# Linear attention and MLP layers in fp32r: operand addresses, warming products, half tiles and a new order

## Chip, cores and metric

One core of a Trainium2 chip. The metric is the device time of one execution in microseconds; the kernel before took 888.67 us (median of three runs, 885.83 to 890.14).

## What is computed

Two layers over x of 2,048 rows and 448 columns, each an attention block A and an MLP block B with the same weights in both layers:

```python
x = x + _A_ref(_layernorm(x), A_wqkv, A_wo)   # 16 heads of 28; phi(t) = (t + 1 if t > 0 else exp(t)) + 1e-6
# q, k, v = x @ wqkv; kv = phi(k).T @ v; z = sum phi(k); o = phi(q) @ kv / (phi(q) . z + 1e-6); o @ wo
x = x + _B_ref(_layernorm(x), B_w1, B_b1, B_w2, B_b2)   # gelu(x @ w1 + b1) @ w2 + b2, 1,792 hidden
```

All of it is float32. Products run on TensorE as fp32r (a rounded fp32); to keep the accuracy each operand is split into a high and a low part, and high x high, high x low and low x high are summed.

## The kernel before, in words

x is cut into 16 tiles of 128 rows. 448 columns are three pieces of 128 and a tail of 64; the tail's high and low parts (of the weights, in `w1x` and pieces 6, W6 for wk and V6 for wq) share one piece of 128 rows. For a projection of one tile, `proj` (L486 on) issues eleven products of 448 columns: for each of three pieces high x high (L492), high x low (L493) and low x high (L494), and two for the tail (L496, L497).

The parts of a layer, by the names that the order uses: `ld` loads a tile of x; `a`, `ar`, `n` are the statistics (DVE), the root (POOL, L349) and the normalization (DVE, L353); `d` copies the tail (ACT); `T` turns a tile by four transposes on TensorE into one bank (`tp`, L382), or `tu`, `st`, `sp` turn it on DVE in 32 x 32 squares, store it to DRAM and load it spread; `xh` and `xl` split the turned tile (ACT and DVE); `sh` and `sl` split the tile as it is (ACT, and POOL at L484 and L485). `K` and `Q` are the projections, with `ke`, `kp`, `kh`, `kl`, `za` and `qe`, `qp`, `qs` behind them (exponentials on ACT, the rest on DVE; `qs` stores phi(q) to DRAM). `G` sums x-transposed times phi(k) over all tiles in four banks (eleven products a tile, L566 to L570). `wkld`, `wkh`, `wkl` and `wqld`, `wqh`, `wql` load and split the pieces of wk and wq; `bld`, `bhi`, `blo` those of w1 and w2 (layer 0 only). Behind the last G come the small products (`z`, `gt`, `kv`, `m`), then per tile the division (`pl`, `pz`, `pd`, `pm`), its turning, `o` or `oc` (products with the combined matrix), the second norm, and the MLP: `f` (eleven products of 512 columns for 128 hidden units and four tiles, L799 to L803), `g`, `gh`, `gl` (gelu and its split), `y` (four times three products of 448 columns, L826 to L828, into four banks over 14 `f`), `ya` and `ys` (sum and store).

The order in which all of this is issued is written out by hand, as a list of these names for each layer (`ORDER`): `run` (L853) goes through it and calls the function of each name, with the tile or piece as number. `:p` or `:a` gives the engine, and `>` or `<` takes the name from the next or the former layer, so the layers overlap. Each engine executes its instructions in that order; every wait between engines follows from the tiles. Loads on SP are one queue, in the same order; a few of the first are issued by ACT (`:a`).

Before the first tile is ready, `warm20` issues 20 transposes of a constant, whose results nobody reads.

Tiles are laid out in SBUF in the order of their pools and first uses, each at a multiple of 32 bytes: constants first (from byte 384), then the weights of the MLP (`wts`), then `work`, in which the small tiles of the statistics stand between the large ones. By the sizes, `w1h` starts at byte 5,696, `w2h` at 55,872, XH at 159,040, the rings A, B, E, F, of 2,048 bytes, at 202,560 and on: 64 bytes over a multiple of 256 in each case. The pieces wk 1, 4 and 6 (142,848 and on) and the rings S and e start at a multiple of 256.

PSUM has eight banks: four with the name `acc` (G, y, o), two `h` (f, Q, transposes) and two `m` (K and the small products).

Of the kernel before, what the change touches and what calls it, by code (L numbers as in the profile page):

```python
# [70 lines left out]
    ),  # L71
    (
# [43 lines left out]
def linear_attn_mlp_kernel(  # L116
# [46 lines left out]
    def small(n, name):  # L163
        return work.tile([128, n], F32, name=name, tag=name, bufs=BUFS["small"])
# [51 lines left out]
    @op  # L216
    def warm(l, n, e):
        if (l, "warm") not in T:
            T[l, "warm"] = bank("m", "warm")
        for i in range(n):  # L220
            pe.transpose(T[l, "warm"][:, :128], ident, ident)
# [668 lines left out]
```

## Time and profile before

| what | us |
|---|---|
| median of three runs | 888.67 |
| the profiled execution | 886.11 |
| its span, first to last instruction | 884.4 |
| TensorE busy in the span | 873.2 |
| DVE busy | 473.7 |
| ACT busy | 337.0 |
| POOL busy | 203.8 |

Busy times of TensorE count pipelined products, so its load is better read from the distance between the starts of consecutive instructions. Other engines' busy times are those of one instruction at a time. A row of the timeline gives start, duration, engine, line, operation, out<-in and shape; PEld is the load of a stationary operand, PE the product itself. A row of the stretches gives, for each engine, busy time and number of instructions, then the granted clock of TensorE, the DMA engines' share and GB/s.

### The profile page before, as it was taken

The numbers are of one execution on the slowest core, as the hardware profiler recorded it, in microseconds if no ns is written. First come the engines' busy times: TensorE is split into PE (matmuls) and PEld (weight loads), VectorE is DVE, ScalarE is ACT, GpSimd is POOL, SyncE is SP. The second block draws the span as 40 slices with busy tenths as digits, with TensorE's granted clock in tenths as the row PEclk, the third lists the DMA queues.
The fourth block names the chain that finished last, engine by engine and source line by source line (L and its number), as shares of the span: only waits on it lengthen the run. The fifth ranks groups of instructions, "written<-read, shape, count | busy, mean of one in ns | idle before, by whom it ended". The sixth has DMA issues, their size and how long they took to land.

```text
span 884.4 us, 11576 instructions
## 1 busy us (share of the span) xinstructions
PE 873.2 (99%) x4184; PEld 773.2 (87%) x4184; DVE 473.7 (54%) x970; ACT 337.0 (38%) x594; POOL 203.8 (23%) x239
## 2 busy tenths in 40 slices
PE   8999999999999999999999999999999999999998
PEld 7999888889888888888889898888888888888887
DVE  6877597456555434225468855853754564342212
ACT  5768644323223222324446554342232232223221
POOL 3656543231022002010033323130320230020000
PEclk9999999999999999999999999999999999999999
DMA  4677623522413241141145453134234124020101
GB/s 138 202 229 229 190 80 120 169 90 84 154 36 117 86 145 48 49 136 48 49 135 175 152 153 105 52 104 146 98 101 152 59 82 135 1 96 1 52 1 42
DMA packets 62762, 93.71 MB, mean 106 GB/s; under 512 B 8816, under 2 KB 57968, under 8 KB 62704
## 3 DMA queue, kind: packets, MB, share of 16 engines
q1 hardware_dynamic: 62096, 92.05, 32.5%
q10 hardware_dynamic: 608, 0.92, 0.3%
q8 instruction: 33, 0.54, 0.3%
q14 instruction: 25, 0.20, 0.1%
HBM read 55.65 MB, written 34.08 MB: 101 GB/s over the span
## 4 chain that ended last, share of the span: by engine, by line
PE 93%; DVE 3%; DMA 2%; ACT 1%; issue 0%; POOL 0%; SPq 0%; ACTq 0%; POOLq 0%; DVEq 0%
PE y L828 10%; PE y L827 10%; PE y L826 10%; PE hp L800 9%; PE hp L799 9%; PE hp L801 9%; PE hp L802 3%; PE hp L803 3%; PE psk L492 2%; PE G L567 2%; PE G L568 2%; PE G L566 2%; PE psk L494 2%; PE psk L493 2%; PE psq L493 2%; PE psq L494 2%
## 5 line engine op out<-in xcount | busy, mean ns | idle before, releaser
L818 DVE TENSOR_TENSOR gl<-g,gh 128x512 fp32r<-128x512 f32 x112 | 80.9, 728 | 193.6 <-ACT gh L210 193.4
L828 PE MATMUL y<-w2h,gl 128*128 128x448 f32 x448 | 163.7, 365 | 1.5 <-DVE gl L818 1.5
L827 PE MATMUL y<-w2l,gh 128*128 128x448 f32 x448 | 163.7, 365 | 0.0
L826 PE MATMUL y<-w2h,gh 128*128 128x448 f32 x448 | 163.6, 365 | 0.0
L808 ACT ACTIVATE g<-hp,b1s 128x512 f32<-128x512 f32 x112 | 76.2, 686 | 201.2 <-PE hp L803 183.8
L210 ACT CAST gh<-g 128x512 fp32r<-128x512 f32 x112 | 69.1, 620 | 171.7 <-PE y L827 158.5
L800 PE MATMUL hp<-XH,w1l 128*128 128x512 f32 x336 | 131.2, 390 | 0.0
L801 PE MATMUL hp<-XL,w1h 128*128 128x512 f32 x336 | 131.1, 390 | 0.0
L799 PE MATMUL hp<-XH,w1h 128*128 128x512 f32 x336 | 131.1, 390 | 0.0
L349 POOL TENSOR_TENSOR brs<-bve,mhalf 128x1 f32<-128x1 f32 x64 | 39.2, 616 | 342.4 <-DVE bve L343 342.3
L828 PEld LDWEIGHTS y<-w2h,gl 128*128 128x128 f32 x448 | 84.2, 188 | 8.5 <-DVE gl L818 1.9
L826 PEld LDWEIGHTS y<-w2h,gh 128*128 128x128 f32 x448 | 84.2, 188 | 8.4
L827 PEld LDWEIGHTS y<-w2l,gh 128*128 128x128 f32 x448 | 84.1, 188 | 8.0
L801 PEld LDWEIGHTS hp<-XL,w1h 128*128 128x128 f32 x336 | 63.1, 188 | 13.5
L800 PEld LDWEIGHTS hp<-XH,w1l 128*128 128x128 f32 x336 | 63.1, 188 | 11.8
L799 PEld LDWEIGHTS hp<-XH,w1h 128*128 128x128 f32 x336 | 63.1, 188 | 11.7
L665 POOL TENSOR_TENSOR pz<-pq,zb 128x448 f32<-128x448 f32 x32 | 38.7, 1212 | 100.2 <-DVE dn L670 57.2
L484 POOL TENSOR_TENSOR xnl<-x,xnh 128x384 fp32r<-128x384 f32 x32 | 33.6, 1051 | 68.3 <-ACT xnh L210 48.0
L744 DVE TENSOR_TENSOR x<-op,x 128x448 f32<-128x448 f32 x32 | 19.8, 620 | 51.6 <-PE op L738 50.8
L420 DVE TENSOR_TENSOR XL<-sp,XH 128x512 fp32r<-128x512 f32 x50 | 35.8, 728 | 18.8 <-ACT XH L210 18.8
L339 DVE BATCH_NORM_STATS2 bst<-x 128x6 f32<-128x448 f32 x64 | 39.7, 620 | 9.3 <-DMA x<-in_A_x_dram 5.7
L802 PE MATMUL hp<-XH,w1x 128*128 128x512 f32 x112 | 43.6, 389 | 0.0
(142 smaller groups left out, 1577.2 us busy)
## 6 DMA issues: line engine op xcount, KB each, us to landing
x<-in_A_x_dram SPq DMA_DIRECT2D x32, 224.0 KB, 4.0
pq_d<-eq SPq DMA_DIRECT2D x32, 224.0 KB, 2.6
pq<-pq_d SPq DMA_DIRECT2D x32, 224.0 KB, 3.2
x<-x_d SPq DMA_DIRECT2D x32, 224.0 KB, 2.9
sq_a<-sq SPq DMA_DIRECT2D x13, 512.0 KB, 2.9
sp<-sq_a SPq DMA_DIRECT2D x52, 128.0 KB, 3.2
sq_q<-sq SPq DMA_DIRECT2D x12, 512.0 KB, 2.9
sp<-sq_q SPq DMA_DIRECT2D x48, 128.0 KB, 2.9
```

The source lines that it names most:

```text
L210: act.copy(out, src)
L339: dve.bn_stats(st, xs)
L349: pool.tensor_tensor(rs, ve, mhalf, op=OP.pow)
L799: pe.matmul(o, w1h[:, c, s], x.moving(x.hi, c), start=(c == 0), stop=False)
L800: pe.matmul(o, w1l[:, c, s], x.moving(x.hi, c), start=False, stop=False)
L801: pe.matmul(o, w1h[:, c, s], x.moving(x.lo, c), start=False, stop=False)
L802: pe.matmul(o, w1x[:, s], x.moving(x.hi, 3), start=False, stop=False)
L808: act.activation(T[l, "g", n], T[l, "hp", n], AF.Gelu_apprx_tanh, bias=b1s[:, n % NF:n % NF + 1])
L818: dve.tensor_sub(lo, T[l, "g", n], f(hi))
L826: pe.matmul(o, gh[:, r], w2h[:, i, s], start=first, stop=False)
L827: pe.matmul(o, gh[:, r], w2l[:, i, s], start=False, stop=False)
L828: pe.matmul(o, gl[:, r], w2h[:, i, s], start=False, stop=last)
```

## The change

- **Addresses.** The small tiles of the statistics move to a pool of their own, and a constant tile of 56 floats that nobody uses is added. By the sizes, `wts` then starts at byte 6,432, and as all its tiles and those of `work` are multiples of 256 long, every one of them starts 32 bytes over a multiple of 256.
- **Warming.** `hot16` stands for `warm20`: 16 products of 512 columns with a tile of ones, whose results nobody reads. `ones` becomes fp32r and is set first on POOL.
- **Halves.** Tiles 0 and 1 of layer 0 are turned, split and projected for K in halves (`ht`, `hx`, `hl`, `hk`) of two pieces each, in place of T, xh, xl and K. Each tile's K keeps its eleven products, in another sequence.
- **`fl`**: one more product like those of `hot`, behind the transposes of tile 5 in layer 0.
- **Order.** Both lists are new throughout. At the start `ar0` stands right behind `a0`; wk's low parts 0, 1 and 2 are on DVE and 3 on POOL (before: 1 on POOL); wq's pieces 1 and 3 are loaded by SP and no longer by ACT. Fewer parts of layer 1 stand in layer 0's list.

```diff
-        "ld0 a0 ld1 a1 wkld0 wkld1:a wkld2 wkld3:a wqld0 wqld1:a wkh1 wkl1:p wkh3 ar0 n0 d0 wkh0 ar1 n1 d1 wkl3 "
-        "warm20 wqld2 ld2 wkl0 T0 xh0 xl0 wkh2 wqld3:a tab0 T1 xh1 wqh0 wqh2 sh0 wkl2 K0 xl1 K1 ke0 a2 ar2 wql0 "
-        "wqh1 wql1:p n2 wql2 d2 T2 kp0 wqh3 wql3 Q0 kh0 kl0 ld4 ld3 a4 a3 ke1 sl0 G0 qe0 qp0 qs0 kp1 kh1 xh2 ar4 "
+        "ld0 a0 ar0 ld1 a1 n0 hot16 wkld0 wkld1:a wkld2 wkld3:a wkh1 wkl1 ht0 wkh0 ar1 wkl0 n1 d0 ht1 hx0 hl0 hk0 "
+        "wkh2 wkl2 wkh3 d1 ht3 hx1 hl1 wqld0 wqh0 ht2 hx2 wkl3:p hk1 hx3 hl2 hk2 hl3 wql0 hk3 ld2 wqld1 wqh1 a2 "
+        "ke0 kp0 bld1:xn wqld2 wqh2 wqld3 wqh3 kh0 sh0 wql2 wql3 wql1:p Q0 ar2 n2 d2 T2 sh1 sl0 kl0 G0 ld3 ld7 a3 "
...
+        "ke4 kp4 Q4 kh4 T5 xh5 sp3 blo4 bhi5 blo5 ar11 fl kl4 qs3 xl5 tu10 n11 a9 za4 tu8 G3 G4 bld6:xn bld7:xn "
...
+        ">wkh0 gh52 gl52 y52 >wkl0 >tu3 >wql0 >sp0 >xh0 gh53 g55 g54 gl53 y53 gh54 >st1 gl54 y54 >sh0 >sl0 >xl0 "
+        ">K0 gh55 gl55 y55 >tu4 >xh1 >xl1 ya13 ya12 >ld5 >sp1 lb14 ya14 ys13 ys12 >ld6 ya15 ys15 "
...
+        "ke0 Q0 K1 Q1 xh2 xh3 kp0 kh0 ke1 xl2 a5 ar5 xl3 n5 za0 tu5 qe0 <ys14 ld7 kl0 G0 a6 sh1 qe1 qp1 ld8 st2 "
...
+    smalls = ctx.enter_context(tc.tile_pool(name="smalls", bufs=2))
...
-        return work.tile([128, n], F32, name=name, tag=name, bufs=BUFS["small"])
+        return smalls.tile([128, n], F32, name=name, tag=name, bufs=BUFS["small"])
...
+    ones = consts.tile([128, 128], F32R, name="ones")
+    pool.memset(f(ones), 1.0)
...
+    consts.tile([128, 56], F32, name="pad")
...
+    @op
+    def hot(l, n, e):
+        w = bank(e or "m", "hot")
+        for i in range(n):
+            pe.matmul(w.rearrange("p (r n) -> p r n", r=4), ones, ones[:, None, :].to_broadcast([128, 4, 128]),
+                      start=True, stop=True)
...
+    def ht(l, n, e):
+        t, h = divmod(n, 2)
+        tp = T["tp", ("h", l, n)] = bank(e or "acc", "tp")
+        for c in (2 * h, 2 * h + 1):
+            pe.transpose(tp[:, rows(c % 2)], T["tail", l, t] if c == 3 else T["xn", l, t][:, rows(c)], ident)
...
+    def fl(l, n, e):
+        hot(l, 1, e)
```

`hx` copies one half's 256 columns (ACT), `hl` subtracts them (DVE). `hk` issues six products for the first half (the four high ones, then the two low ones) and five for the second.

More of the change, by code (lines that the diff above doesn't have):

```diff
@@ L177, in linear_attn_mlp_kernel @@
     pool.memset(zc, S * 1e-6)
-    ones = consts.tile([128, 128], F32, name="ones")
-    pool.memset(ones, 1.0)
     mask = consts.tile([G, G], F32, name="mask")
@@ L452, in tu, with hx, hl, hk @@
     @op
+    def ht(l, n, e):
[3 more added lines that the diff above has]
+            pe.transpose(tp[:, rows(c % 2)], T["tail", l, t] if c == 3 else T["xn", l, t][:, rows(c)], ident)
+    @op
+    def hx(l, n, e):
+        t, h = divmod(n, 2)
+        copy(ENG[e or "a"], block("a", l, t // 4).pieces(t % 4)[0][:, h * 256:(h + 1) * 256],
+             T["tp", ("h", l, n)][:, :256])
+    @op
+    def hl(l, n, e):
+        t, h = divmod(n, 2)
+        hi, lo = (x[:, h * 256:(h + 1) * 256] for x in block("a", l, t // 4).pieces(t % 4))
+        dve.tensor_sub(lo, T["tp", ("h", l, n)][:, :256], f(hi))
+    @op
+    def hk(l, n, e):
+        t, h = divmod(n, 2)
+        if h == 0:
+            T["K", l, t] = bank(e or "m", "psk")[:, :D]
+        o = T["K", l, t]
+        b = block("a", l, t // 4)
+        if h == 0:
+            for c in range(2):
+                for w in range(2):
+                    pe.matmul(o, b.still(b.hi, t % 4, c), T[l, "w", "k", c][w], start=(c + w == 0), stop=False)
+            for c in range(2):
+                pe.matmul(o, b.still(b.lo, t % 4, c), T[l, "w", "k", c][0], start=False, stop=False)
+        else:
+            pe.matmul(o, b.still(b.hi, t % 4, 2), T[l, "w", "k", 2][0], start=False, stop=False)
+            pe.matmul(o, b.still(b.hi, t % 4, 2), T[l, "w", "k", 2][1], start=False, stop=False)
+            pe.matmul(o, b.still(b.hi, t % 4, 3), T[l, "w", "k", 3], start=False, stop=False)
+            pe.matmul(o, b.still(b.lo, t % 4, 2), T[l, "w", "k", 2][0], start=False, stop=False)
+            pe.matmul(o, b.still(b.lo, t % 4, 3), T[l, "w", "k", 3], start=False, stop=True)
+    @op
+    def fl(l, n, e):
+        hot(l, 1, e)
+    @op
     def tu(l, t, e):
@@ L587, in z @@
         T[l, "zp"] = bank(e or "m", "zp")[:, :D]
-        pe.matmul(T[l, "zp"], ones, T["za", l], start=True, stop=True)
+        pe.matmul(T[l, "zp"], f(ones), T["za", l], start=True, stop=True)
     @op
```

171 rows, old and new, of the table ORDER are left out of this document.

## The prediction

> **What bounds the kernel now.** I read the page's shares first, then PE's waits, then the starts of PE's instructions in the timeline, since the shares alone say only "PE".
>
> ```profile
> span 884.4 us, 11576 instructions
> PE 873.2 (99%) x4184; PEld 773.2 (87%) x4184; DVE 473.7 (54%) x970; ACT 337.0 (38%) x594; POOL 203.8 (23%) x239
> PE 93%; DVE 3%; DMA 2%; ACT 1%; issue 0%; POOL 0%; SPq 0%; ACTq 0%; POOLq 0%; DVEq 0%
> ```
>
> TensorE is busy 99% and holds 93% of the chain that ended last. It hardly waits: the longest waits on the page of PE's waits are
>
> ```profile
> PE tp L382 <- DVE x L353: 2.8, 1, 2.8
> PE y L828 <- DVE gl L818: 1.5, 1, 1.5
> PE psk L492 <- DVE za L538: 0.8, 1, 0.8
> PE psq L492 <- DVE eq L507: 0.6, 1, 0.6
> ```
>
> 5.7 us in all, half of it before the first projection. So a gain has three places: the start, the few waits, and the distance from one product's start to the next. Four stretches of the timeline give that distance.
>
> ```profile
> 21.29 0.37 PE L492 MATMUL psq<-wq,XH 128*128 128x448 f32 x1
> 23.52 0.36 PE L492 MATMUL psk<-wk,XH 128*128 128x448 f32 x1
> ...
> 65.42 0.37 PE L492 MATMUL psq<-wq,XH 128*128 128x448 f32 x1
> 67.70 0.37 PE L492 MATMUL psk<-wk,XH 128*128 128x448 f32 x1
> 69.94 0.36 PE L492 MATMUL psk<-wk,XH 128*128 128x448 f32 x1
> ...
> 465.57 0.36 PE L492 MATMUL psq<-wq,XH 128*128 128x448 f32 x1
> 467.80 0.36 PE L492 MATMUL psk<-wk,XH 128*128 128x448 f32 x1
> 500.46 0.37 PE L492 MATMUL psq<-wq,XH 128*128 128x448 f32 x1
> 505.01 0.37 PE L566 MATMUL G<-kh,xnh 128*128 128x448 f32 x1
> ...
> 299.69 0.39 PE L799 MATMUL hp<-XH,w1h 128*128 128x512 f32 x1
> 300.39 0.39 PE L799 MATMUL hp<-XH,w1h 128*128 128x512 f32 x1
> 302.20 0.36 PE L826 MATMUL y<-w2h,gh 128*128 128x448 f32 x1
> 305.24 0.39 PE L799 MATMUL hp<-XH,w1h 128*128 128x512 f32 x1
> ```
>
> The same 11 products of a Q take 2.23 us at 21.29 (203 ns each) and 2.28 us at 65.42 (207 ns). There are two steady states: a free one and a **slow lock**. Layer 1 has both too: 2.23 us at 465.57, and 22 products in 4.55 us at 500.46. The K between 67.70 and 69.94 takes 2.24 us. The 15 products of y up to 305.24 take 3.04 us, 203 ns: free. A product of 512 columns starts 233 ns after the last one at first (three in 0.70 us), then 226 (eight in 1.81 us). Free, it costs some 13 ns over its columns (512 are 213 at 2.4 per ns: twice the half-clock rate of the cold rows under the rivals); a 448-column product costs 16 (187 are columns), locked 20. The weight load beside them says why the short ones cost more:
>
> ```profile
> 65.42 0.19 PEld L493 LDWEIGHTS psq<-wq,XH 128*128 128x128 f32 x1
> 65.63 0.37 PE L493 MATMUL psq<-wq,XH 128*128 128x448 f32 x1
> 305.25 0.19 PEld L800 LDWEIGHTS hp<-XH,w1l 128*128 128x128 f32 x1
> 305.47 0.39 PE L800 MATMUL hp<-XH,w1l 128*128 128x512 f32 x1
> ```
>
> Each load starts as the product before it starts, runs 0.19 us, and its own product follows 0.02 us later at 448 columns, 0.03 us at 512. At 448 the load and its hand-over are the bound, at 512 the stream. Without the load's share a 448-column product would start every 200 ns (187 + 13).
>
> **The addresses (the unknown).** Worked out from the tiles' sizes, w1, w2, XH, XL, A, B, E, F, wq and wk 0, 2, 3, 5 now start 64 bytes over a multiple of 256, and wk 1, 4, 6 and the S and e rings at a multiple. Afterwards all start 32 over: the pad and the constants end there, the small tiles fill 512 bytes of their own, and every large tile is a multiple of 256 long. Nothing in this trace starts 32 over, so the price is bounded from rows. The K at 67.70 holds five products with wk 1, 4, 6 at offset 0, the locked Q before it none: 2.24 against 2.28 us. So the offset matters to a locked product, by 40 ns / 5 = 8 ns at most. A free K doesn't show it (from 21.29 on Q and K alike run at 203). Lower end: no 448-column product is bound by its load, 200 ns for 2,760 of them (1,344 y, 360 op, 1,056 psk, psq and G), and the lock is gone. Upper end: every product locked, 207 and 233 ns. I take the middle between 203 and 200 for the plateau, since offsets 0 and 64 are equally near to 32, and the lock gone, since a locked product is where an offset shows:
> - plateau: 2,760 x 1.35 ns = **-3.7 us**;
> - lock: by the starts in between, read in the same way, it holds from 31 to 108 us and from 474 to 541, 145 us or 700 products; a K loses 10 ns and a Q or G 50 ns in 11, on average 37 / 11 = 3 ns: **-2.1 us**;
> - hp: 112 blocks of 11; the block at 299.69 takes 2.51 us, 11 x 226 are 2.49; half of that difference, as the next block is better: **-1.1 us**.
>
> Together -6.9 us; the ends are -12 (2,760 x 2.7 ns + 2.1 + 2.2) and +14 (1,704 x 4 ns + 1,056 x 2 + 1,232 x 4).
>
> Stores and loads of the S ring move from offset 0 to 32 too. The row first, and where it stands on a chain:
>
> ```profile
> sq_a<-sq SPq DMA_DIRECT2D x13, 512.0 KB, 2.9
> ...
> 467.60 5.10 DMA sq_a<-sq
> ```
>
> The Trainium skill, "DMA: Bandwidth & Descriptors", section "How a descriptor splits into AXI transactions", speaks against the change: a transfer is cut at multiples of 256 bytes, so a 4,096-byte row begun 32 over needs 17 pieces instead of 16. By it the one at 467.60 would grow by at most a sixteenth, 0.3 us (an estimate), once, at the layer boundary; no run here shows it. Without it I price them at nothing: most others (x, w) are off a multiple in both kernels.
>
> **The start.**
>
> ```profile
> 5.22 0.63 DVE L339 BATCH_NORM_STATS2 bst<-x 128x6 f32<-128x448 f32 x1 [0.18 <-DMA x<-in_A_x_dram]
> 6.55 1.13 POOL L286 TENSOR_TENSOR wk<-stg,wk 128x448 fp32r<-128x448 f32 x1 [4.06 <-ACT wk L210]
> 7.64 1.14 POOL L349 TENSOR_TENSOR brs<-bve,mhalf 128x1 f32<-128x1 f32 x2
> 8.22 1.10 DVE L353 TENSOR_SCALAR x<-x,bmv,brs 128x448 f32<-128x448 f32 x2 [1.97 <-POOL brs L349]
> 8.77 0.30 ACT L210 COPY tail<-x 128x128 f32<-128x128 f32 x1 [0.54 <-DVE x L353]
> 9.64 0.58 ACT L210 CAST XH<-tp 128x512 fp32r<-128x512 f32 x1
> 10.27 0.74 PE L492 MATMUL psk<-wk,XH 128*128 128x448 f32 x1
> 16.38 0.49 PE L382 MATMUL tp<-ident,x 128*128 128x128 f32 x3
> 17.13 1.42 POOL L484 TENSOR_TENSOR xnl<-x,xnh 128x384 fp32r<-128x384 f32 x1
> 19.05 0.36 PE L566 MATMUL G<-kh,xnh 128*128 128x448 f32 x1
> 6.50:9.93 3.43, 1.14 (x8) 0.90 (x8) 1.60 (x3) 2.29 (x6) 2.22 (x3) 1.00 1.04 395
> 9.93:13.34 3.41, 3.31 (x9) 2.41 (x9) 3.31 (x9) 2.81 (x7) 0.00 (x0) 0.50 0.29 83
> ```
>
> Today the root of tile 0 (L349) stands on POOL behind a weight's low part (6.55, 1.13 us), so x is normalized at 8.22. The new order puts ar0 right behind a0, whose statistics end before the second ones begin at 5.22, and gives that low part to DVE: the root is done before 6, n0 follows the second statistics (5.22 + 1.0) at 6.3 and is done at 6.8. hot16, 16 products of 512 columns at half clock (0.43 us each), holds PE from 1.1 to about 7.3; the half transposes follow, the half copy on ACT (0.39 us, between 0.30 for 128 and 0.58 for 512 columns) ends at 8.1, and DVE's two low parts (0.62 each, behind n0) at 8.0. So the first half product starts at 8.1 instead of 10.27. The second half needs wkh3 and POOL's wkl3 (1.26 us), near 10.5; K0 and K1 end near 13.9 instead of 16.4. G0 is next to be late: its third product needs sl0, 1.42 us on POOL behind sh0, which now stands behind wqh2, wqh3 and kh0 on ACT; I get 17.7 for it against some 18.6 now, and G0 ends 1 to 2 us earlier. **-1.5 us**, between -2.7 (K1's gain kept) and +1 (ACT and DVE, each with four half operations for two, +0.4 us, run late further on). wqld1 and wqld3 go from ACT's queue to SP's, behind ld2 and bld1; their pieces of 224 KB are needed after 11 us, so they cost nothing while the queue keeps its pace.
>
> The clock rows: 9.93 to 13.34 is granted only 0.50, after PE was busy 1.14 of 3.43 us; the next stretch is full again, after 3.31 of 3.41. The Trainium skill, "TensorE: Matmul & The Clock Gate", Part 1, has this rule: a window of some 3.4 us decides the next one. The trace agrees. By it the halves, which fill some 2.5 of the 3.4 us, may or may not keep the next window full; the sum would be -2.7 us with it kept.
>
> **The rest.** fl is one more 512-column product, 0.2 us: **+0.2**. Its bank is that of K3, whose readers stand ahead of K4 in the order, 4.9 us of PE work earlier, so it waits for nothing; G3 and G4 stand behind it. Behind transposes the next product starts late anyway (tile 5's stood before a G today), so fl can also carry the stream out of the lock, which the lock's term holds already. At the layer boundary the waits at psq and psk (0.6 + 0.8, and their slow restarts, 2.0 us) are DVE's. In the new order Q0, K1 and Q1 (3 x 2.23 = 6.7 us) follow y55, while DVE does two of four ya, kp0, xl2, a5, xl3, n5, za0, tu5 and kl0, some 6.9 us, before G0: even. I take half of the 2.0 us: **-1.0**, ends -2 and +2. The tail (y55, ya, ys) is the same. Small tiles in a pool of their own, the pad and the earlier memset of ones add nothing but addresses.
>
> **Sum.** The profiled execution took 886.1 us (1.7 outside its span), 2.6 under the median of 888.67. 886.1 - 6.9 - 1.5 + 0.2 - 1.0 = **876.9 us**.
>
> **Rivals.**
> - *Only equal offsets matter.* Both operands of a product are at 64 today and at 32 then: the same distance, the same states. For it: wk 1, 4, 6, which differ from their stationary operand, are the exception in the lock; y at equal offsets is free. Then the 6.9 us stay: 883.8.
> - *The other side: locked everywhere.* The states lie 4 ns apart (203 and 207) with nothing between, so a product seems to wait for a step. If operands are read in pieces of 64 bytes (every start is a multiple of 64 today), one begun 32 bytes into a piece takes a piece more, at load and stream; from some 4 ns on, the load's hand-over (0.02 us) slips to the next step, and y falls into the state of 65.42. Price +14, with start and boundary unchanged: 886.1 + 14 - 2.3 = 898. Against it: at 0 the lock is weaker, not stronger.
> ```profile
> 11.83 0.57 PE L492 MATMUL psk<-wk,XH 128*128 128x448 f32 x1
> 12.95 0.55 PE L492 MATMUL psk<-wk,XH 128*128 128x448 f32 x1
> ```
>
> - *The whole gap goes.* The three products from 11.83 on take 0.37 us each, their columns alone at half clock; at full clock that would be 187 ns, some -60 us, 825. Nothing warm comes near it.
> - *The order is worse*: if the S ring's tiles 4 and 5 reach K4 late, PE waits at the boundary as now or twice as long, and the start is cold: 889.
>
> **Chances.** Forecast (870 to 881.7) 0.48; below 0.05; equal offsets (882 to 887) 0.28, a sixth of it under 881.7; worse order 0.06; locked 0.13. About 0.5% is what a measurement of this kernel can tell from no change: 881.7 and 890.5. Faster 0.55, same 0.26, slower 0.19. The range goes from 868 to 891: it leaves out the locked case and the whole gap, some 0.17.
>
> **What would show it.** psk L492's first start near 8 us; a granted clock of 1.00 in the window after; psq, psk and G between 31 and 108 us at 2.23 us in 11; y's 15 products in under 3.02 us; hp's first three at 0.68. If y's distance stays 203 ns, the plateau term is wrong; if it is 207, the other side is right. New rows among PE's waits would charge the order.

## The result, and the profile after

The changed kernel takes 879.86 us (median of five runs, 879.64 to 881.13) beside 886.24 for the kernel before (five runs, 885.83 to 890.14, the three of the table above among them): a ratio of 0.9919, 95% interval 0.9898 to 0.994. The profiled execution took 880.06 us. Lines of its page, then of its page of PE's waits:

```profile
span 878.3 us, 11548 instructions
PE 873.2 (99%) x4181; PEld 772.4 (88%) x4181; DVE 473.7 (54%) x972; ACT 336.4 (38%) x596; POOL 202.6 (23%) x239
PE 99%; DVE 0%; ACT 0%; issue 0%; POOL 0%; POOLq 0%
```

```profile
PE hot L228 <- POOL ones L170: 1.1, 1, 1.1
PE psk L489 <- ACT XH L211: 0.2, 1, 0.2
PE tp L465 <- ACT tail L211: 0.2, 1, 0.2
```

The span is 6.1 us shorter, PE is as busy as before, and it now holds 99% of the chain that ended last, not 93%. Of the four waits that the prediction quotes from before, 5.7 us in all, none is left; 0.4 us of new ones behind `hot` have come. PE's timeline at the start, in the first projections and at the layer boundary:

```profile
7.17 0.49 PE L465 MATMUL tp<-ident,x 128*128 128x128 f32 x3
8.01 1.08 PE L489 MATMUL psk<-wk,XH 128*128 128x448 f32 x4 [0.24 <-ACT XH L211]
13.54 0.37 PE L543 MATMUL psq<-wq,XH 128*128 128x448 f32 x1
16.16 0.45 PE L617 MATMUL G<-kh,xnh 128*128 128x448 f32 x1
16.65 0.37 PE L619 MATMUL G<-kh,xnl 128*128 128x448 f32 x1
...
40.01 0.48 PE L228 MATMUL hot<-ones 128*128 128x512 f32 x1
40.33 0.37 PE L617 MATMUL G<-kh,xnh 128*128 128x448 f32 x1
...
85.78 0.37 PE L543 MATMUL psk<-wk,XH 128*128 128x448 f32 x1
88.06 0.36 PE L617 MATMUL G<-kh,xnh 128*128 128x448 f32 x1
...
491.85 0.37 PE L621 MATMUL G<-kl,xnh 128*128 128x448 f32 x1
492.25 0.44 PE L543 MATMUL psk<-wk,XH 128*128 128x448 f32 x1
```

The first product starts at 8.01 and the first G at 16.16 (before: 10.27 and 19.05). But the K from 85.78 to 88.06 takes 2.28 us for 11 products, 207 ns each: the slow lock is still there. The table adds up the starts of all PE instructions behind the first psk. Distances under 245 ns between 448- or 512-column products are steady; "pitch" is what they hold above (or below) the free 202.66 and 226.67 ns, "waits" is what the longer distances hold above them (products at half rate are among these), "other" the distances behind transposes, `fl`, the plain fp32 products z and m and the small products. The free distances themselves are 838.4 us in every kernel, so the first four columns and 838.4 give the last one.

| kernel | first psk | pitch | waits | other | last product starts |
|---|---|---|---|---|---|
| before | 10.27 | 3.25 | 7.99 | 20.52 | 880.43 |
| after | 8.01 | 3.15 | 2.76 | 22.12 | 874.43 |
| all at 64 (e1) | 7.82 | 3.03 | 3.25 | 22.02 | 874.52 |
| all at 0 (e2) | 7.78 | 2.12 | 4.07 | 22.09 | 874.45 |
| before, at 32 (e3) | 10.31 | 2.10 | 8.67 | 20.52 | 880.00 |
| operands apart (e4) | 7.69 | 2.79 | 3.42 | 22.10 | 874.39 |
| apart, f equal (e5) | 8.19 | -0.35 | 3.39 | 22.09 | 871.71 |
| before, root first (e6) | 9.78 | 2.87 | 10.12 | 20.57 | 881.74 |
| warm20 (e7) | 7.96 | 2.89 | 4.75 | 21.72 | 875.71 |
| whole tiles (e8) | 10.39 | 2.91 | 2.83 | 21.29 | 875.82 |
| whole, K0 first (e9) | 8.65 | 2.73 | 4.50 | 22.54 | 876.81 |
| no fl (e10) | 7.99 | 2.48 | 5.96 | 21.77 | 876.59 |
| before, f early (e11) | 10.42 | 3.38 | 6.30 | 20.52 | 879.01 |
| before, apart (e12) | 10.56 | -0.63 | 10.67 | 20.51 | 879.51 |

From before to after: 2.26 us from the first product, 5.23 from waits, 0.10 from the pitch, and 1.60 lost in "other": 0.96 behind transposes, of which the half transposes that now stand behind the first psk hold 0.81, 0.32 behind `fl`, and 0.3 behind the products between G and the MLP. The change moved the pitch by next to nothing; its gain is the start's and the order's.

### The profile page after: what moved, and what is told of

It reads as the page before. It is cut to its first block, busy times and chain, and to the rows that moved or that the text cites. A ratio compares the mean times of both kernels' runs of the same rounds, so it can differ in the third digit from the quotient of the medians.

```text
span 878.3 us, 11548 instructions
## 1 busy us (share of the span) xinstructions
PE 873.2 (99%) x4181; PEld 772.4 (88%) x4181; DVE 473.7 (54%) x972; ACT 336.4 (38%) x596; POOL 202.6 (23%) x239
## 4 chain that ended last, share of the span: by engine, by line
PE 99%; DVE 0%; ACT 0%; issue 0%; POOL 0%; POOLq 0%
PE y L878 10%; PE y L879 10%; PE y L877 10%; PE hp L851 9%; PE hp L852 9%; PE hp L850 9%; PE hp L854 3%; PE hp L853 3%; PE G L618 2%; PE psq L543 2%; PE G L617 2%; PE G L619 2%; PE psq L545 2%; PE psq L544 2%; PE psk L543 2%; PE psk L545 2%
## 5 line engine op out<-in xcount | busy, mean ns | idle before, releaser
L357 POOL TENSOR_TENSOR brs<-bve,mhalf 128x1 f32<-128x1 f32 x64 | 41.0, 642 | 318.7 <-DVE bve L351 317.6
L854 PE MATMUL hp<-XL,w1x 128*128 128x512 f32 x112 | 43.6, 389 | 0.0
```

Of the source, the lines that this page charges most:

```text
L357: pool.tensor_tensor(rs, ve, mhalf, op=OP.pow)
L854: pe.matmul(o, w1x[:, s], x.moving(x.lo, 3), start=False, stop=True)
```

## Experiments: the addresses

Theory: the offset itself is worth nothing; the slow lock belongs to products whose two operands start at equal offsets, and begins by an accident of timing. Rival, the prediction's view: a start at a multiple of 256 or at 32 over it is better than one at 64.

**e1 and e2**, the kernel after with the pad 32 bytes longer or shorter:

```diff
-    consts.tile([128, 56], F32, name="pad")
+    consts.tile([128, 64], F32, name="pad")     # e1; e2: 48
```

> The kernel after with the pad made 64 floats, so that every large tile starts 64 bytes over a multiple of 256, all alike. Theory (the order made the gain; equal offsets are all the same): y's 15 products in 3.04 us as before and after, 879.9 us within 0.2%. Rival (32 itself is worth something): 1 us or more slower, or another distance in y, psq or hp.

> The kernel after with the pad made 48 floats, every large tile at a multiple of 256. Theory: as with 64, 879.9 us within 0.2%. Rival (an absolute offset matters, as the K with wk 1, 4, 6 at 0 suggested in the kernel before): the locked Q, K and G run at 203 instead of 207 ns, 1 us or more faster.

Measured: 880.17 us (0.9915 of before, 0.9896 to 0.9933) and 879.83 (0.9913, 0.9892 to 0.9933), like the kernel after. In time, all operands at 64, at 32 or at 0 are the same. At 0 the lock stayed away in most of layer 0 (pitch 2.12 for 3.15), and waits gave it all back (4.07 for 2.76). That this is an accident and no merit of 0 is argued, not shown; but at 32 the pitch also runs from 2.10 (e3) to 3.15.

**e3**, the kernel before with the change's addresses alone (small tiles in their own pool, the pad).

> The kernel before with only the addresses of the one after (small tiles in a pool of their own, and the pad), its order untouched. Theory: ratio to before 1.000 within 0.2%; the locked K loses its exception for wk 1, 4, 6 and runs at 2.28 us in 11 instead of 2.24, 32 K, at most 0.8 us slower. Rival (addresses are part of the gain): 1 us or more faster than before.

Measured: 888.02 us beside 887.21, ratio 1.0005 (0.9991 to 1.0019). So the prediction's 6.9 us for the addresses did not come on either kernel: the interval allows 0.8 us of gain at most. The locked K lost its exception, as expected (206 ns from 31.40 us on); the profiled execution has less lock in all (pitch 2.10 for 3.25), and the time does not show it.

**e4**, the kernel after with XH, XL, A and B 64 bytes further, so that the operands of every large product differ by 64 bytes:

```diff
+    stat = ctx.enter_context(tc.tile_pool(name="stat", bufs=1))
...
-        return work.tile([128, n], dt, name=name, tag=tag, bufs=BUFS.get(tag, 1))
+        return (stat if tag in ("XH", "XL", "A", "B") else work).tile([128, n], dt, name=name, tag=tag, bufs=BUFS.get(tag, 1))
...
+    stat.tile([128, 16], F32, name="spad")
```

> The kernel after with XH, XL and the rings A and B, the stationary operands of K, Q, G and y and the moving one of f, in a pool of their own 96 bytes over a multiple of 256, all others still 32 over: the two operands of a product 64 bytes apart, as wk 1, 4, 6 and XH were in the kernel before. Theory (only the distance of the two operands matters, and only to a locked product): Q, K and G between 45 and 88 us at 2.23 instead of 2.28 us in 11, hp's first three nearer to 0.68 than 0.70, 1 to 3 us faster than after. Rival (the lock has nothing to do with addresses): no change.

Measured: 880.72 us, 0.9921 (0.9903 to 0.9939): the theory's 1 to 3 us did not come, for there are two effects against each other. psk, psq and G have no lock (their pitch falls from 1.63 to -0.38 us) and y takes 202.2 ns for 202.7 (-0.6), while hp, the products of `f`, loses 2.2 us: its 112 blocks of 11 take 2.527 us on average for 2.507.

**e5** keeps hp's operands equal and sets only the 448-column products' apart: A and B at 96, the rings of wk and wq at 224, XH, XL, w1 and w2 at 32.

```diff
+    ab = ctx.enter_context(tc.tile_pool(name="ab", bufs=1))
+    wv_ = ctx.enter_context(tc.tile_pool(name="wv_", bufs=1))
...
-        return work.tile([128, n], dt, name=name, tag=tag, bufs=BUFS.get(tag, 1))
+        p = ab if tag in ("A", "B") else wv_ if tag[0] in "WV" else work
+        return p.tile([128, n], dt, name=name, tag=tag, bufs=BUFS.get(tag, 1))
...
+    ab.tile([128, 16], F32, name="pad1")
+    wv_.tile([128, 32], F32, name="pad2")
```

> The kernel after, with A and B 64 bytes further (96 over a multiple of 256) and the rings of the weights' pieces at 224, while XH, XL, w1 and w2 stay at 32: the two operands of every 448-column product lie 64 bytes apart (or -64), those of hp stay equal. Theory (the slow lock needs equal offsets of the two operands, and hp is good at equal offsets): no lock in psk, psq and G (their 1.6 us over 202.66 ns gone), y at 202.3 as with the operands apart (-0.6), hp at 227.9 as in the kernel after: 877.8 us, -2.0 to -2.2 against the kernel after. Rival (hp was worse with the operands apart for another reason, such as the products of 448 columns before it leaving another phase): hp at 229 to 230 again, and the time at 880 to 880.7. Second rival (a lock is an accident of each layout): lock in other places, 879 to 881.

Measured: **877.5 us** (877.37 to 877.9, four runs), 0.9897 of before (0.9881 to 0.9912); all four runs lie below all five of the kernel after. The theory's number was 877.8. PE's timeline of this kernel, a K at the place of the locked one above and a block of hp:

```profile
84.96 0.37 PE L548 MATMUL psk<-wk,XH 128*128 128x448 f32 x1
87.18 0.36 PE L622 MATMUL G<-kh,xnh 128*128 128x448 f32 x1
...
299.78 0.39 PE L855 MATMUL hp<-XH,w1h 128*128 128x512 f32 x1
302.27 0.37 PE L882 MATMUL y<-w2h,gh 128*128 128x448 f32 x1
```

The K takes 2.22 us for 2.28, the block 2.49. Of hp's 112 blocks 90 take 2.49 us, 44 in the kernel after: the unlocked products in front seem to leave hp in its better pattern more often. This is the fastest version found.

**e12** makes the same layout for the kernel before; the order is untouched.

> The kernel before, with small tiles and pad as in the change and with the operands of the 448-column products 64 bytes apart while those of hp stay equal (as in the kernel of that name built from after); the order untouched. Theory (the slow lock and the last 0.3 ns of a y product need equal offsets, whatever the order): psk, psq and G free at 202 ns all along, y at 202.3, hp's excess near 0.75 us instead of 1.3, together 2.4 to 2.6 us off the sum of the distances and off the time: 884.5 beside 887.0, with the same spread of some 4 us. Rival (it is the new order's phases that made it work): lock in layer 0 as before, 886.5 to 887.

Measured: 885.03 us beside 887.53, 0.9976 (0.9961 to 0.9991). The lock is gone here too (pitch -0.63 for 3.25, 3.9 us), so it is the layout and not the new order's timing that does it. By the medians the old order gains 2.5 us from it (0.8 to 3.5), as expected and as much as the new order does (2.4, e5). The two profiled executions lie only 0.9 us apart, for the waits column grew by 2.7 us. Two of PE's waits are part of that:

```profile
PE y L835 <- DVE gl L825: 1.6, 1, 1.6
...
PE psk L499 <- DVE za L545: 1.3, 1, 1.3
```

The waits at y and psk, 1.5 and 0.8 us before, are 1.6 and 1.3; the first projections at half rate take 0.4 us more, and the rest is spread over small late starts. A faster PE that reaches DVE's results earlier would do this, but one execution of each kernel doesn't show it, and the medians don't.

## Experiments: the order and the start

Theory: the start is a chain through POOL, ACT, DVE and PE, in which each part of the new start counts; the waits of before were the order's alone. Rivals stand with each run.

**e6**, the kernel before with the roots of tiles 0 and 1 right behind their statistics:

```diff
-        "ld0 a0 ld1 a1 wkld0 wkld1:a wkld2 wkld3:a wqld0 wqld1:a wkh1 wkl1:p wkh3 ar0 n0 d0 wkh0 ar1 n1 d1 wkl3 "
+        "ld0 a0 ar0 ld1 a1 ar1 wkld0 wkld1:a wkld2 wkld3:a wqld0 wqld1:a wkh1 wkl1:p wkh3 n0 d0 wkh0 n1 d1 wkl3 "
```

> The kernel before, with the roots of tiles 0 and 1 right behind their statistics, ahead of the weight's low part on POOL; nothing else. Theory (the start is a chain through several engines, so the root alone moves the limit on to ACT): n0 is done at 6.8 instead of 8.8, but the tail's copy stands behind the two casts of wk's piece 3 on ACT, which end at 8.2, and XH behind that, wkh0 and the second tail: first psk at 9.7 instead of 10.27, -0.5 us against the kernel before. Rival (the root on POOL is the whole delay, as the prediction's start says): first psk near 8.3, -2.0 us. The runs' spread of some 5 us with the granted clock stays in both, as the 20 transposes stay.

Measured: 887.42 us beside 887.07, ratio 1.0003 (0.9991 to 1.0015): the rival's 2.0 us are ruled out, the theory's 0.5 can't be told from nothing. ACT, then PE:

```profile
7.81 0.56 ACT L210 CAST wk<-stg 64x448 fp32r<-64x448 f32 x1
8.28 0.29 ACT L210 COPY tail<-x 128x128 f32<-128x128 f32 x1
```

```profile
8.63 0.47 PE L382 MATMUL tp<-ident,tail 128*128 128x128 f32 x1 [0.97 <-ACT tail L210]
...
9.78 0.74 PE L492 MATMUL psk<-wk,XH 128*128 128x448 f32 x1
10.31 0.57 PE L493 MATMUL psk<-wk,XH 128*128 128x448 f32 x1
...
13.68 0.57 PE L497 MATMUL psk<-wk,XL 128*128 128x448 f32 x1
14.05 0.49 PE L492 MATMUL psk<-wk,XH 128*128 128x448 f32 x1
```

The root alone moves the first product from 10.27 to 9.78, as the theory said: the tail's copy then stands behind ACT's casts of wk's piece 3. In this execution the whole K0 ran at half rate as well (0.37 us a product to 14.05).

**e7**, the kernel after with `warm20` in place of `hot16`.

> The kernel after, with the 20 transposes in place of the 16 products of 512 columns. They end near 6.0 instead of 7.3, so PE is busy some 0.8 us less in the window 6.50:9.93 (2.95 us in the kernel after). Theory (the long products keep that window full, and with it the clock of the next): first psk still near 8.0, but the next window at 0.50 in the profiled execution or in some of the runs, the runs spread over some 3 to 5 us again with mean clocks of 0.995 to 1.00 as those of the kernel before do, median 881 to 882. Rival (the half tiles alone fill the window): 880 with a spread of 1 to 2 us and a clock of 1.00.

Measured: 881.34 us (880.76 to 882.82), 0.9941 (0.9928 to 0.9953), 1.5 us over the kernel after: the theory's time, with less than its spread. The first psk starts at 7.96, but PE runs at half rate up to 10.4; beside it the warming products of the kernel after (a row of x4 counts those that start in the window asked for, the one at 5.91 among them):

```profile
6.81 0.90 PE L465 MATMUL tp<-ident,x 128*128 128x128 f32 x3 [0.72 <-DVE x L361]
7.66 0.47 PE L465 MATMUL tp<-ident,tail 128*128 128x128 f32 x1
7.96 1.86 PE L489 MATMUL psk<-wk,XH 128*128 128x448 f32 x4
9.62 0.95 PE L491 MATMUL psk<-wk,XL 128*128 128x448 f32 x2
10.36 0.35 PE L465 MATMUL tp<-ident,x 128*128 128x128 f32 x1
```

```profile
4.63 1.76 PE L228 MATMUL hot<-ones 128*128 128x512 f32 x4
5.91 1.42 PE L228 MATMUL hot<-ones 128*128 128x512 f32 x5
```

Three of `hot` start in the 1.28 us from 4.63 to 5.91, 427 ns each, then five in the 1.26 us up to 7.17: the clock comes while they run. The 20 transposes end sooner, and the clock came only at 10.4. K1 is done 0.6 us later than in the kernel after, and the last product starts 1.3 us later; the waits column, half-rate products included, is 4.75 for 2.76.

**e8**, the kernel after with T, xh, xl and K whole for tiles 0 and 1:

```diff
-        "ld0 a0 ar0 ld1 a1 n0 hot16 wkld0 wkld1:a wkld2 wkld3:a wkh1 wkl1 ht0 wkh0 ar1 wkl0 n1 d0 ht1 hx0 hl0 hk0 "
-        "wkh2 wkl2 wkh3 d1 ht3 hx1 hl1 wqld0 wqh0 ht2 hx2 wkl3:p hk1 hx3 hl2 hk2 hl3 wql0 hk3 ld2 wqld1 wqh1 a2 "
+        "ld0 a0 ar0 ld1 a1 n0 hot16 wkld0 wkld1:a wkld2 wkld3:a wkh1 wkl1 wkh0 ar1 wkl0 n1 d0 T0 xh0 xl0 "
+        "wkh2 wkl2 wkh3 d1 T1 xh1 wqld0 wqh0 wkl3:p K0 xl1 wql0 K1 ld2 wqld1 wqh1 a2 "
```

> The kernel after, with tiles 0 and 1 turned, split and projected whole, in the same order of the engines otherwise. Theory (a half saves the half of one copy and one transposition ahead of the first product, and POOL's low part of piece 3 limits K0 anyway): first psk at 8.35 instead of 8.01, K1 starts at 11.4 to 11.6 instead of 11.26, +0.3 to +0.5 us: 880.3. Rival (halves carry the start): first psk near 9.3, the window after at 0.50, +1.3 us or more: 881.2 or above.

**e9**, the same with K0 ahead of tile 1's transposes: `wkh2 wkl2 wkh3 wkl3:p K0 d1 T1 xh1 wqld0 wqh0 xl1 wql0 K1` in the second line.

> The kernel after, with tiles 0 and 1 whole again, but with K0 ahead of tile 1's transposes on PE (with the transposes ahead of it, psk started at 10.39). Theory (what the half tiles bring is mostly that tile 0's products need not stand behind tile 1's transposes): first psk at 8.4, its last products at 10.8 behind POOL's low part of piece 3, K1 at 11.3 to 11.5 and done at 13.7 to 13.9, against 13.5 in the kernel after: +0.2 to +0.4 us, 880.2. Rival (the halves themselves carry the start): K1 done at 14.5 or later, or half-rate products behind the gap: 881 or above.

Measured: 881.45 us (0.9947, 0.9934 to 0.9959) and 882.32 us (0.9941, 0.9924 to 0.9959): 1.6 and 2.5 us over the kernel after, and in the profiled executions the last product starts 1.4 and 2.4 us later than there. Both numbers of the theory were too small; the rivals' times came. PE's timeline of e8, then of e9:

```profile
8.35 0.55 PE L390 MATMUL tp<-ident,x 128*128 128x128 f32 x3 [0.56 <-DVE x L361]
10.31 0.33 PE L390 MATMUL tp<-ident,tail 128*128 128x128 f32 x1 [1.41 <-ACT tail L211]
10.39 0.45 PE L543 MATMUL psk<-wk,XH 128*128 128x448 f32 x1
```

```profile
8.65 0.47 PE L543 MATMUL psk<-wk,XH 128*128 128x448 f32 x1 [0.68 <-ACT XH L211]
11.50 0.49 PE L390 MATMUL tp<-ident,x 128*128 128x128 f32 x3
...
12.77 0.47 PE L543 MATMUL psk<-wk,XH 128*128 128x448 f32 x1 [0.68 <-ACT XH L211]
```

With T1 ahead of K0 (e8), K0 waits 1.41 us for a tail that it doesn't need, behind ACT's casts; I had overlooked that order in my expectation. With K0 ahead of T1 (e9), the trip from transposes through ACT's copy to the first product lies open twice, 0.68 us each time. The halves let PE work on one half while the other is copied, so K1 is done at 13.5 instead of 14.9 and 15.4. What halves bring is this cover, 1.4 to 1.9 us, not the shorter copy.

**e10**, the kernel after without the unread product `fl`.

> The kernel after, without fl, the one unread product behind tile 5's transposes. Theory (fl is only one more product; its distance to the next is 0.32 us): 879.6, the G behind the transposes starting 0.2 to 0.3 us earlier and the slow lock somewhere else or as long as before. Rival (fl shields the product behind the transposes from a slow first start): that G starts 0.1 to 0.35 us late, 879.9 and no difference. Second rival (fl sets the phase and so the lock): the lock from 40 to 88 us is gone, -0.9 us.

Measured: 881.71 us (880.56 to 883.39), 0.9931 (0.9913 to 0.995); two of its six runs are as short as the kernel after. Every theory missed something. The lock from 40 to 88 us is gone (0.16 us of pitch between 14 and 111 us for 1.06): in this execution it was `fl` behind which the lock began. But the time is not shorter, for DVE fell behind (in the profiled execution; the waits column is 5.96 for 2.76). DVE and POOL of this kernel, then PE's wait, then DVE's three instructions in the kernel after:

```profile
43.08 1.36 DVE L361 TENSOR_SCALAR x<-x,bmv,brs 128x448 f32<-128x448 f32 x1 [0.80 <-POOL brs L357]
...
46.51 1.57 DVE L428 TENSOR_TENSOR XL<-sp,XH 128x512 fp32r<-128x512 f32 x1
48.01 1.20 DVE L361 TENSOR_SCALAR x<-x,bmv,brs 128x448 f32<-128x448 f32 x1
```

```profile
46.38 1.16 POOL L339 TENSOR_TENSOR w1l<-stg,w1h 128x448 fp32r<-128x448 f32 x1 [0.38 <-ACT w1h L211]
47.51 1.46 POOL L535 TENSOR_TENSOR xnl<-x,xnh 128x384 fp32r<-128x384 f32 x1
```

```profile
PE G L618 <- DVE kl L580: 1.1, 1, 1.1
```

```profile
43.12 0.51 DVE L361 TENSOR_SCALAR x<-x,bmv,brs 128x448 f32<-128x448 f32 x1 [0.79 <-POOL brs L357]
...
45.71 0.65 DVE L428 TENSOR_TENSOR XL<-sp,XH 128x512 fp32r<-128x512 f32 x1
46.28 0.51 DVE L361 TENSOR_SCALAR x<-x,bmv,brs 128x448 f32<-128x448 f32 x1
```

The first of them, at 43.08, meets a subtraction that POOL starts at 43.17 and takes 0.85 us longer; in the kernel after, POOL starts it only at 43.49. So DVE comes late to the next two. They take 1.16 us in the kernel after, where POOL's next subtraction starts only at 46.70, and 2.77 when they meet POOL's subtractions: XL ends 0.54 us after POOL's w1l does (47.54 to 48.08), nearly as though it had begun there. A shift of a few tenths decides whether they meet. So how `fl` is priced can't be told from one place: it costs 0.32 us where it stands, and moves everything behind it.

**e11**, the kernel before with f6 moved from behind y2 to ahead of gl1 and y1:

```diff
-        "f3 u2 u0 gl1 y1 pd5 pm5 pu4 pu5 g4 gh2 gh4 mc ld7 pl6 blo25 pz6 pd6 gl2 y2 f6 pl7 pz7 ps2 g3 gh3 gl4 gl3 "
+        "f3 u2 u0 f6 gl1 y1 pd5 pm5 pu4 pu5 g4 gh2 gh4 mc ld7 pl6 blo25 pz6 pd6 gl2 y2 pl7 pz7 ps2 g3 gh3 gl4 gl3 "
```

> The kernel before, with f6 moved from behind y2 to ahead of gl1 and y1, so that one more block of eleven products lies ahead of the y that waits for gl1. Theory (that wait, 1.5 us and its slow restart, is a matter of the order alone, and one block of 2.5 us covers it): no y line on the page of PE's waits, -1.7 us against the kernel before, 885.3 beside 887.0. Rival (the wait only moves): f6 or a later y waits as long, 887.

Measured: 885.26 us beside 887.53, 0.997 (0.9959 to 0.9982). PE's waits no longer name y (the lines left out are those of the warming and, at the end, of tq):

```profile
PE tp L382 <- DVE x L353: 2.7, 1, 2.7
...
PE psq L492 <- DVE eq L507: 0.6, 1, 0.6
PE psk L492 <- DVE za L538: 0.3, 1, 0.3
```

One name moved takes the wait away, with nothing late in its place. The waits column falls by 1.7 us, the median by 2.3 (the theory: 1.7). The spread falls too: the twelve runs lie within 1.3 us (884.53 to 885.8), those of the kernel before beside them within 5.5 (884.5 to 890.04).

## Why the prediction was right, and where it was wrong

The time forecast, 876.9, is 3.0 us under the time measured, and faster was right. But the gain was 6.4 us where 9.2 were forecast, and it came by other terms than the sum named: that it came so near is luck.

- **The pitch, -6.9: wrong, measured -0.1.** The failing step is "the middle between 203 and 200 for the plateau" with "the lock gone, since a locked product is where an offset shows". That wk 1, 4 and 6 at offset 0 ran 8 ns better in the lock was read as a merit of offset 0. By the runs it was a merit of differing from the other operand (e4, e5, e12). At equal offsets 64, 32 and 0 give the same time (e1, e2, e3). The rival of equal offsets had the mechanism; its 883.8 fell with the other terms. The lock's term was real: setting operands apart, which the change doesn't do, ends the lock and gains 3.5 us of pitch (e5), 2.0 of them in psk, psq and G. The plateau of 200 ns was not: y's best is 202.2.
- **The start, -1.5: right in kind, too small, measured -2.9 at the first G.** First psk at 8.1 (8.01 came), K1 done at 13.9 (13.54), G0's third product at 17.7 (16.65). sl0 was not the limit that I made of it, and K1's gain, which the forecast had kept in part, was kept whole. The clock was there for it: the profile after shows the windows

```profile
6.50:9.93 3.43, 2.95 (x16) 2.13 (x15) 2.63 (x6) 3.06 (x8) 1.46 (x2) 1.00 1.06 376
9.93:13.34 3.41, 3.41 (x19) 3.14 (x20) 2.85 (x8) 3.35 (x9) 2.01 (x3) 1.00 1.06 330
```

  with PE busy 2.95 us and a clock of 1.00 behind it, where before had 0.50. The rule of the Trainium skill ("TensorE: Matmul & The Clock Gate", Part 1), by which the sum would have been -2.7, agrees with these rows; its case with the next window kept full is the one that came. But the bounds are those of the kernel before: in the trace after, the record of the clock, from which the column is made, begins with a full grant at 6.08 us, while `hot` still runs, and does not fall before the last instruction. So the warming brought the clock, and the halves had only to keep it. How full a window must be for that, no run here shows: with whole tiles (e8) PE was busy for only 1.74 us between 6.50 and 9.93, and the products behind it still start 0.20 us apart.
- **The boundary, -1.0: right in kind, measured -1.6 in the two profiles; no run tests it alone.** Two late starts at 460.0 and 487.9, 0.77 and 1.01 us over the pitch, became one of 0.20 (491.85 to 492.25 in the rows above, less 0.20).
- **The wait of y at L828, 1.5: seen and not priced.** The prediction quoted the row and gave it no term. It went with the new order (-1.8 with the slow start behind it), and e11 shows that moving one name does it. With the 1.4 us that the start brought beyond its term, the 0.6 of the boundary and the restarts below, this omission made up for more than half of the 6.8 us that the pitch did not bring.
- **`fl`, +0.2: right at its place (0.32), wrong in its effect.** It was to help the stream out of the lock; the lock begins behind it, at 40.33.
- **Restarts, not priced.** The plain fp32 products z and m stood ahead of projections or a G, which then started slowly (0.55 us to the next) at four places; now at one, -1.05 us. Small slow starts elsewhere gave back 0.7.
- **The transfers.** The profile's row for the store of the S ring is now

```profile
sq_a<-sq SPq DMA_DIRECT2D x13, 512.0 KB, 3.0
```

  3.0 us for 2.9. The Trainium skill ("DMA: Bandwidth & Descriptors", section "How a descriptor splits into AXI transactions") would allow up to 0.3 more, worked out as an estimate in the prediction; the row moved by 0.1, and none of PE's waits names such a transfer, so pricing it at nothing held.
- **The chances** do not add up exactly: their parts give 0.58 for faster, not 0.55, and the worse order's 889 lies under the 890.5 from which slower was counted.

What stays open: why equal offsets of the two operands allow the lock and why hp prefers them; whether any distance but 64 bytes does the same, and whether 256 is the step that counts (the only distance run was 64); what starts a lock; and whether `fl` is worth its place in the fastest layout, where the lock did not occur. None of that was run.

## What to carry to other kernels

Before giving an offset a price, ask whether the rows show the offset of one operand or the distance between two: change all by the same amount first. When PE waits nowhere for long, list every wait and every slow restart with its price and give each a term, for a hand-written order can remove them one by one. A faster stream can run into the engines that feed it: look at the waits column beside the pitch, and at the medians of many runs before two profiled executions are compared (e12: 0.9 us between the profiles, 2.5 between the medians).

## What the runs showed of the hardware

- **Two operands' relative offset matters to steady fp32r products.** With both at the same offset modulo 256, 448-column products run at 202.66 ns or, for stretches of tens of us, at 206.7; 64 bytes apart nearly all blocks of 11 run at 201.6 to 202.7 (e4, e5, e12), with none of those stretches. 512-column products do the opposite: 2.527 us in 11 with the operands apart (e4), 2.507 or 2.500 with them equal.
- **DVE and POOL hold each other up.** 0.65 and 0.51 us became 1.57 and 1.20 beside POOL (e10). It is not rare: of the 64 normalizations in the kernel after, the 47 that meet no POOL instruction of over 0.9 us take at most 0.52 us, and 13 of the other 17 take 0.82 to 1.36. The Trainium skill, "SBUF — State Buffer", section "🔬 SBUF: two separate sides", calls the port pair of these two an exclusive lock held for an instruction; the end of XL 0.54 us after POOL's w1l, near its own 0.65, agrees. The x behind it ends only 0.24 us after POOL's xnl (48.97 to 49.21), less than its own 0.51, so that the lock lasts for the whole instruction is not shown for that one.
- **The granted clock's column misses the start.** The rows of e6 and e7 show 1.00 for the windows in which the products are 373 ns apart:

```profile
6.50:9.93 3.43, 3.12 (x9) 2.49 (x10) 2.70 (x6) 3.04 (x9) 1.50 (x2) 1.00 1.06 371
```

  Above is e7's window, with the first psk from 7.96 on in it. The records of the clock in these traces begin only with the first full grant, at 10.53 us in e7 and 14.31 in e6, and the column counts what lies ahead of them as 1.00; the mean clock of a run does so too. In the first 14 us the distance between products is the better witness.
- **The kernel before spreads, the new one hardly does.** Its runs lie between 884.5 and 890.8 us with mean clocks from 0.994 to 1.000, those of the kernel after between 879.6 and 881.1 at 0.999 to 1.000. The half-rate stretch at the start does not explain most of it: e11 keeps that start and has mean clocks from 0.996 to 1.000, yet its runs lie within 1.3 us; and two runs of the kernel before with the same mean clock, 0.998, took 884.5 and 890.04. In e11 the spread went with the wait of y; how long that wait is in the slower runs, no trace here shows.
